# Eleven zero matmuls instead of 27 in the first gaps of TensorE

## The chip, the cores and the metric

The kernel runs on one core of one Trainium2 chip. The metric is the device time of one execution in microseconds. The core has five instruction streams: TensorE (PE; its weight loads are shown as PEld), VectorE (DVE), ScalarE (ACT), GpSimd (POOL) and SyncE (SP), which issues nearly all transfers here.

## What is computed

```
scores  = scale * x @ state^T          a  = softmax(scores)      xread = a @ state
scores2 = scale * state @ x^T          a2 = softmax(scores2)     sread = a2 @ x
y   = concat([xread, sread]) along the sequence, heads side by side   # 8 x (512 + 32) rows, 512 wide
out = maximum(y @ w1, y @ w2) @ w_out
```

There are 8 batches, 8 heads, 512 rows of x and 32 of state for each, 64 numbers a head; w1 and w2 are 512 x 1024, w_out is 1024 x 512. Inputs and output are f32, the products run in bf16.

## The kernel before, in words

maximum(h1, h2) is written as h2 + relu(h1 - h2). So the kernel forms w1 - w2 (the tile wd) and w2 @ w_out (the tile wwo) once, and multiplies both with the state of each batch (sw), so that the attention's probabilities (at) meet products of state and weights rather than the weights. For each batch of x there follow the first layer (l1, line 375), relu, and the second layer in quarters by a scheme of sums and differences (lines 426 and 432).

Weights, x and state come in pieces that SP issues in a fixed order: `ldx.b.g` is half of a batch of x, `ldw1.k`, `ldw2.k` and `ldwo.k` are quarters of the weights, each 256 x 512 numbers. The quarters that matter here come in the order ldw2.2, ldw2.3, ldwo.2, ldw1.3, ldwo.3, ldw1.2, ldw2.1, ldw2.0, ldwo.0, ldwo.1, ldw1.0, ldw1.1.

The first part of the program is an order written out by hand: the string ORDER, a list of tokens. Each token is one step on one engine, `name.args@banks` for TensorE with the PSUM banks that it writes, `name.args>engine` for the others. The loop that reads it issues one step after the other, so the order of the tokens on an engine is the order of its instructions. The steps that the text speaks of:

- `fill.k@bank`: one matmul of a tile of zeros (wz) into a bank. Nothing reads its result. With k of 100 and more it is 512 columns wide, else 256.
- `xt`, `S`, `at`: transposes of x (line 249), of the state (line 208) and of the probabilities a (line 291); `sc` are the scores (line 264), `srw` the state's read (line 321).
- `cwo`, `cw2`: casts of loaded weights to bf16; `w2` transposes a piece of w2 (line 548); `ww` is a part of w2 @ w_out (line 606).
- `sub.k.h`: half a piece of w1 - w2 (line 560); `sw.b.z` multiplies a part of wd or wwo with the state of batch b (line 352), and `swe` takes the result from its bank (line 102 on ACT, line 104 on DVE).

```
fill=lambda k, r: idle(1, r, 512 if k >= 100 else 256, k >= 200)

def idle(n, ring, w=512, f32=False):
    p = bank(ring)
    z = wz.bitcast(F32)[:, 0:256] if f32 else wz[:, 0:w]
    for j in range(n):
        nc.tensor.matmul(p[:, 0:z.shape[1]], z[:, 0:128], z, start=True, stop=True)
```

A matmul is two instructions in TensorE's stream, LDWEIGHTS and MATMUL. After the listed part, loops over the batches follow, which the change leaves as they are.

Of the kernel before, what the change touches and what calls it, by code (L numbers as in the profile page):

```python
# [20 lines left out]
CHUNKS = [[(0, 512), (512, 1024)], [(0, 512), (512, 1024)]]  # L21

ORDER = """
ldx.0.0 ldS.0.2 fill.10@0 ldx.0.1 fill.109@1 ldx.1.1 fill.114@0 fill.11@1 ldx.1.0 fill.110@0 ldw2.2 fill.100@1
fill.9@0 ldw2.3 fill.111@1 ldwo.2 fill.0@0 fill.5@1 fill.101@0 ldw1.3 ce.0.1>A ce.0.0>V ldwo.3 xt.0.0@0 cS.0.2>V
ldw1.2 fill.106@1 xte.0.0>V fill.105@2 ce.0.3>P ce.0.2>A ldw2.1 S.0.2@1 xt.0.1@2 ldw2.0 Se.0.2.1>A Se.0.2.0>V sc.0.0@1
xte.0.1>V fill.13@0 ldwo.0 fill.6@3 ce.1.2>P exp.0.0>A fill.115@4 fill.108@3 sc.0.1@4 ce.1.3>V ldwo.1 red.0.0>V
exp.0.1>A xt.1.1@3 ce.1.0>A ce.1.1>P srw.0@4,1 xte.1.1>V ldw1.0 mul.0.0>P swre.0.0>A red.0.1>V sc.1.1@3 xt.1.0@2
cw2.2>P exp.1.1>A ldw1.1 fill.15@4 fill.107@0 xte.1.0>V fill.1@4 swre.0.1>A fill.2@3 fill.14@0 fill.3@4 fill.112@3
cw2.3>A red.1.1>V mul.0.1>P fill.102@4 fill.7@3 ldx.2.0 fill.4@2 mul.1.1>V w2.3@2 cwo.2>A w2.2@3 w2e.3>V sc.1.0@4  # L30
at.0.0@0 at.0.1@1 exp.1.0>A w2e.2>V ww.3.2@2 ldx.2.1 ww.2.2@4 red.1.0>V sub.3.1>P ate.0.0>A srw.1@3,5 ate.0.1>A
mul.1.0>V cwo.3>A ww.0.2@1 sub.3.0>V at.1.0@0 at.1.1@6 swre.1.0>A ww.1.2@7 sub.2.0>V ate.1.1>A ldS.2.8 ww.3.3@2
ww.1.3@7 sub.2.1>V ate.1.0>A ww.0.3@1 swre.1.1>A sw.1.1@0,6 sw.0.1@5,3 swe.1.1.0>A swe.1.1.1>V ww.2.3@4 swe.0.1.0>A
swe.0.1.1>V l1.1.5@6 cw2.1>P srp.0>P srp.1>P l1.1.7@0 cw2.0>A re.1.5>V l1.0.7@3 w2.1@5 re.1.7>V re.0.7>A w2.0@6 w2e.1>V cwo.0>A
l1.0.5@3 l1.1.6@0 w2e.0>V l1.1.4@5 cwo.1>A ww.2.0@4 re.0.5>V ww.1.0@7 re.1.4>A ww.2.1@4 sub.0.0>V ww.1.1@7 re.1.6>A
sub.0.1>V ww.3.0@2 wwe.2>A ww.0.1@1 sub.1.1>V ww.3.1@2 wwe.1>A ww.0.0@1 sub.1.0>V wwe.3>A l1.0.4@7 wwe.0>A cb.2.0>P
sw.0.0@2,4 re.0.4>V wt.0>P sw.1.0@0,5 swe.0.0.0>A swe.0.0.1>V sw.0.w@1,3 sw.1.w@7,6 cb.2.1>P swe.1.0.0>A swe.1.0.1>V xtd.2 wt.1>P
p2.1@2 l1.0.6@4 swe.0.w.0>A re.0.6>V l1.0.3@0 l1.0.2@5 swe.0.w.1>A re.0.3>V swe.1.w.0>V mS.1>A
l1.0.1@4 l1.0.0@1 p2.0@3 swe.1.w.1>V mS.0>A Sd dif.0>P re.0.2>V re.0.1>A re.0.0>A p2o.0
l1.1.0@7 l1.1.1@6 l1.1.2@0 l1.1.3@5 re.1.0>V re.1.1>A re.1.2>A rs.0.0>V rs.0.1>V re.1.3>A  # L40
p2o.1 ldx.4.1 ldx.3.0 ldx.4.0 ldx.3.1
p1.0@1 k0.0>A p1.1@4 rs.0.2>V wt.2>V v00.0 p6.0 rs.0.3>V k0.1>A k1.0>A p5.0@7 wt.3>V v00.1 rs.1.0>V k2.0>A
sc.2.0@6 exp.2.0>A sc.2.1@0 exp.2.1>A sw.2.0@5,3 red.2.0>V mul.2.0>P red.2.1>V swe.2.0.0>A swe.2.0.1>A ce.2.0>A ce.2.1>A ce.2.2>A ce.2.3>A
p7.0 o7.0 v11.0 rs.1.1>V mul.2.1>P p3.0 o3.0 rs.1.2>V atd.2 sw.2.w@6,2 swe.2.w.0>A v01.0 swe.2.w.1>A
p4.0 o4.0 rs.1.3>V ce.3.0>P ce.3.1>P cb.3.0>P ce.3.2>P ce.3.3>P cb.3.1>P v10.0>A store.0 xtd.3 dif.1>P
sr.2@0 p6.1 k1.1>A sw.2.1@5,3 sre.2>V swe.2.1.0>A swe.2.1.1>V p5.1@7 k2.1>A
p7.1 o7.1 v11.1 p3.1 o3.1 v01.1 srt.2@0 srte.2>A p4.1 o4.1 v10.1>A ldx.5.0 ldx.5.1
"""

LATE = 2  # L50
# [851 lines left out]
```

## Time and profile before

| | |
|---|---|
| median of 3 runs | 145.04 us (145.03 to 145.11) |
| profiled execution | 144.88 us, of which 143.1 us from the first to the last instruction |
| mean granted clock of TensorE | 0.996 |
| PE busy | 134.7 us, 94% of the span |
| transfers | 29.50 MB, mean 206 GB/s |

The profile's times count from the first instruction. A row of the timeline reads: start, busy time, engine, line, operation, out<-in, shapes, count, and in brackets the idle time of the engine before it with what ended it. The chain of waits is followed back from the last instruction, and lists start, duration and work. In the rows of windows, an engine has its busy time and in brackets its count of instructions.

### The profile page before, as it was taken

The page shows a single profiled execution, that of the slowest core. Times are in us where ns is not written, and L with a number is a line of the kernel's source. Part 1 is how long each engine was busy: PE and PEld are TensorE (multiplying, and loading weights), DVE is VectorE, ACT ScalarE, POOL GpSimd, SP SyncE. Part 2 cuts the span into 40 slices and gives each one's busy share as a digit, 9 for nine tenths or more (in the row PEclk, how much of TensorE's full clock was granted, in tenths as well). Part 3 has the DMA queues.
Part 4 walks back from the last instruction along what each step waited for, and adds up shares of the span by engine and source line. Part 5 has one row for each costly group of instructions (what it writes and reads, how often), then busy time and mean ns, then how long its engine had stood idle before and what let it go on. Part 6 is the DMA issues. An engine that isn't in the chain of part 4 may idle for free.

```text
span 143.1 us, 3680 instructions
## 1 busy us (share of the span) xinstructions
PE 134.7 (94%) x1448; PEld 95.4 (67%) x1458; DVE 108.3 (76%) x197; ACT 86.9 (61%) x168; POOL 72.1 (50%) x99
## 2 busy tenths in 40 slices
PE   6889989999999999999999999999999999999980
PEld 2467725456787776786778477747876786788860
DVE  3488959868999938997899799669948997847420
ACT  4367589895689535855682769086726855753220
POOL 4147326099009993399269908971990464200000
PEclk9999999999999999999999999999999999999998
DMA  3999999945997979949995999759137042502073
GB/s 112 342 366 392 384 386 386 343 83 93 196 343 230 286 180 249 236 42 293 242 386 109 212 355 195 160 213 211 35 65 293 2 58 82 234 5 73 9 248 119
DMA packets 36452, 29.50 MB, mean 206 GB/s; under 512 B 22608, under 2 KB 32336, under 8 KB 35536
## 3 DMA queue, kind: packets, MB, share of 16 engines
q1 hardware_dynamic: 36160, 29.10, 70.8%
q8 instruction: 12, 0.20, 0.6%
q10 hardware_dynamic: 272, 0.13, 0.3%
q14 instruction: 8, 0.07, 0.1%
HBM read 15.20 MB, written 8.91 MB: 169 GB/s over the span
## 4 chain that ended last, share of the span: by engine, by line
PE 83%; DMA 11%; ACT 1%; issue 1%; DVE 0%; SPq 0%; DVEq 0%
PE bank L426 36%; PE bank L375 19%; PE bank L432 10%; DMA big<-in_moe_w_out_dram 8%; PE bank L352 5%; DMA big<-in_x_dram 4%; PE bank L606 3%; PE bank L473 2%; PE bank L515 2%; PE bank L264 2%; PE bank L304 2%; PE bank L513 1%; ACT wo L102 1%; PE bank L548 1%; PE bank L336 0%
## 5 line engine op out<-in xcount | busy, mean ns | idle before, releaser
L102 ACT COPY big<-bank 128x512 f32<-128x512 f32 (+2 forms) x40 | 21.9, 551 | 16.6 <-PE bank L426 8.4
L280 POOL TENSOR_TENSOR a<-e,er 128x512 bf16<-128x512 bf16 x14 | 16.7, 1209 | 29.5 <-ACT e L272 18.0
L370 DVE TENSOR_SCALAR r<-bank 128x512 bf16<-128x512 f32 x32 | 21.9, 690 | 11.7 <-PE bank L375 10.6
L375 PE MATMUL bank<-at,sw 128*128 128x512 bf16 x120 | 29.1, 379 | 0.6 <-DVE sw L104 0.2
L426 PEld LDWEIGHTS <-big 128*128 128x128 bf16 x256 | 23.9, 98 | 6.3 <-DVE er L277 2.1
L426 PE MATMUL bank<-big,big 128*128 128x256 bf16 x192 | 23.1, 273 | 0.1
L102 ACT CAST sw<-bank 128x512 bf16<-128x512 f32 x36 | 20.1, 608 | 3.2 <-PE bank L352 3.2
L375 PEld LDWEIGHTS <-sw 128*128 128x128 bf16 x128 | 12.2, 98 | 13.5 <-ACT sw L102 0.5
L368 ACT ACTIVATE r<-bank 128x512 bf16<-128x512 f32 x32 | 18.3, 597 | 4.9 <-PE bank L375 4.7
L426 PEld LDWEIGHTS <-r 128*128 128x128 bf16 x192 | 18.2, 98 | 3.8 <-issue 0.5
L402 DVE TENSOR_TENSOR big<-bank,big 128x512 f32<-128x512 f32 (+1 forms) x25 | 16.4, 660 | 5.4 <-PE bank L432 5.4
L106 POOL CAST xe<-big 128x512 bf16<-128x512 f32 x23 | 16.5, 749 | 6.1 <-DMA big<-in_x_dram 6.1
L426 PE MATMUL bank<-wo,r 128*128 128x256 bf16 x128 | 16.3, 273 | 0.0
L102 ACT COPY sread_t<-bank 128x128 bf16<-128x128 bf16 x8 | 3.2, 472 | 18.7 <-PE bank L336 15.5
L106 POOL CAST xb<-big 128x1024 bf16<-128x1024 f32 x12 | 12.2, 1035 | 4.7 <-DMA big<-in_x_dram 4.7
L432 PE MATMUL bank<-sw,at 128*128 128x256 bf16 x96 | 14.4, 273 | 0.0
L432 PEld LDWEIGHTS <-at 128*128 128x128 bf16 x128 | 12.5, 98 | 1.7
L402 DVE TENSOR_TENSOR big<-r 128x1024 bf16<-128x1024 bf16 x16 | 12.6, 788 | 0.6
L276 DVE TENSOR_REDUCE sums<-e 128x16 f32<-128x512 bf16 x16 | 10.6, 660 | 0.3 <-ACT e L272 0.2
L272 ACT ACTIVATE e<-bank 128x512 bf16<-128x512 f32 x16 | 8.9, 601 | 1.3 <-PE bank L264 1.3
L402 POOL TENSOR_TENSOR big<-sw 128x512 bf16<-128x512 bf16 x8 | 9.2, 1151 | 0.9 <-POOL a L280 0.9
L104 DVE CAST sw<-bank 128x512 bf16<-128x512 f32 x12 | 7.9, 679 | 0.6 <-PE bank L352 0.6
(100 smaller groups left out, 188.7 us busy)
## 6 DMA issues: line engine op xcount, KB each, us to landing
big<-in_x_dram SPq DMA_DIRECT2D x14, 512.0 KB, 6.2
out_dram<-big SPq DMA_DIRECT2D x7, 1024.0 KB, 5.3
big<-in_moe_w_dram SPq DMA_DIRECT2D x8, 512.0 KB, 12.0
big<-in_moe_w_out_dram SPq DMA_DIRECT2D x4, 512.0 KB, 11.6
big<-in_x_dram SPq DMA_DIRECT2D x1, 1024.0 KB, 6.9
out_dram<-big SPq DMA_DIRECT2D x4, 256.0 KB, 2.6
sf<-in_state_dram SPq DMA_DIRECT2D x1, 384.0 KB, 10.4
out_dram<-w2m SPq DMA_DIRECT2D x2, 128.0 KB, 2.5
```

What stands on the lines that cost most here:

```text
L102: nc.scalar.copy(o, i)
L104: nc.vector.tensor_copy(o, i)
L106: nc.gpsimd.tensor_copy(o, i)
L272: nc.scalar.activation(out=e_view(e_s[b % 2], hh).rearrange("p (g c) i n -> p g c (i n)", g=2), in_=p.rearrange("p (c g m) -> p g c m", c= ...
L276: nc.vector.tensor_reduce(es_all[:, b, hh], e_view(e_s[b % 2], hh), axis=AXX, op=ALU.add)
L280: (nc.gpsimd if eng == "P" else nc.vector).tensor_mul(e_view(a_s[b % 2], hh), e_view(e_s[b % 2], hh), er_s[b % 2][:, hh].unsqueeze(3).to_b ...
L368: nc.scalar.activation(out=o, in_=p, func=ACTF.Relu)
L370: nc.vector.tensor_scalar(o, p, scalar1=0.0, scalar2=None, op0=ALU.max)
L375: nc.tensor.matmul(p, sw_s[b % 3][:, g, f * 128:(f + 1) * 128], at_s[b % 3][:, g].rearrange("p c t -> p (c t)"), start=(g == 0), stop=(g = ...
L402: (nc.gpsimd if eng == "P" else nc.vector).tensor_tensor(o, i0, i1, op=op)
L426: nc.tensor.matmul(pv[c], lhs[:, f, 128 * c:128 * c + 128], rhs[:, f, :], start=first and f == 0 and (c == 0 or pv.split), stop=False, ski ...
L432: nc.tensor.matmul(pv[c], at_s[b % 3][:, g, 2 * i + c, :], rhs[:, g, :], start=False, stop=False, skip_group_check=True)
```

## The change

The order has eleven fills instead of 27, all of 512 columns: eight ahead of the first transposes of x (before: eleven, of both widths), none between these and the state's (before: two), one between the scores (before: four), and two instead of ten ahead of the transposes of the first pieces of w2. All other tokens stand in the same order, and the streams of the other engines are unchanged. The first lines of the table:

```
-ldx.0.0 ldS.0.2 fill.10@0 ldx.0.1 fill.109@1 ldx.1.1 fill.114@0 fill.11@1 ldx.1.0 fill.110@0 ldw2.2 fill.100@1
+ldx.0.0 ldS.0.2 fill.100@0 ldx.0.1 fill.101@1 ldx.1.1 fill.102@0 fill.103@1 ldx.1.0 fill.104@0 ldw2.2 fill.105@1
...
```

In TensorE's stream, the last gap: between the transposes of x (xe1) and those of w2 (wb1 is the cast piece) stood, before, ten fills; the first ones and the last one are shown.

```order
L249 MATMUL bank2_65<-ident0_71,xe1_85 128x128
L575 LDWEIGHTS wz0_73
L575 MATMUL bank4_67<-wz0_73 128x256
L575 LDWEIGHTS wz0_73
L575 MATMUL bank0_63<-wz0_73 128x512
...
L575 MATMUL bank2_65<-wz0_73 128x256
L548 LDWEIGHTS wb1_108
```

Now there are two there (the numbers of the lines are three lower, since the table is three lines shorter):

```order
L246 MATMUL bank2_65<-ident0_71,xe1_85 128x128
L572 LDWEIGHTS wz0_73
L572 MATMUL bank3_66<-wz0_73 128x512
L572 LDWEIGHTS wz0_73
L572 MATMUL bank4_67<-wz0_73 128x512
L545 LDWEIGHTS wb1_108
```

Eight matmuls, 16 instructions, are gone from between the two; another eight are gone from the gaps ahead.

The 256th instruction: before, it was the first weight load of the product w2 @ w_out (w2m0 is the transposed w2), just behind the transposes of the probabilities of batch 0 (a0).

```order
L291 LDWEIGHTS a0_93
L291 MATMUL bank1_64<-ident0_71,a0_93 128x128
L606 LDWEIGHTS w2m0_80
L606 MATMUL bank2_65<-wo0_77,w2m0_80 128x512
L606 LDWEIGHTS w2m0_80
```

Now it is among the transposes of batch 1's probabilities (a1), behind the third group of the weight product:

```order
L603 LDWEIGHTS w2m0_80
L603 MATMUL bank1_64<-wo0_77,w2m0_80 128x512
L288 LDWEIGHTS a1_94
L288 MATMUL bank0_63<-ident0_71,a1_94 128x128
L288 LDWEIGHTS a1_94
```

The boundary of 256 has moved by 32 instructions of the work, over four matmuls of the weight product, the state's read of batch 1, two more of the weight product and two transposes.

More of the change, by code (lines that the diff above doesn't have):

```diff
@@ L23 @@
 ORDER = """
-ldx.0.0 ldS.0.2 fill.10@0 ldx.0.1 fill.109@1 ldx.1.1 fill.114@0 fill.11@1 ldx.1.0 fill.110@0 ldw2.2 fill.100@1
[L25 to L44, printed above, removed]
@@ L45 @@
-p4.0 o4.0 rs.1.3>V ce.3.0>P ce.3.1>P cb.3.0>P ce.3.2>P ce.3.3>P cb.3.1>P v10.0>A store.0 xtd.3 dif.1>P
-sr.2@0 p6.1 k1.1>A sw.2.1@5,3 sre.2>V swe.2.1.0>A swe.2.1.1>V p5.1@7 k2.1>A
-p7.1 o7.1 v11.1 p3.1 o3.1 v01.1 srt.2@0 srte.2>A p4.1 o4.1 v10.1>A ldx.5.0 ldx.5.1
+ldx.0.0 ldS.0.2 fill.100@0 ldx.0.1 fill.101@1 ldx.1.1 fill.102@0 fill.103@1 ldx.1.0 fill.104@0 ldw2.2 fill.105@1
+fill.106@0 ldw2.3 fill.107@1 ldwo.2 ldw1.3 ce.0.1>A ce.0.0>V ldwo.3 xt.0.0@0 cS.0.2>V ldw1.2 xte.0.0>V ce.0.3>P
+ce.0.2>A ldw2.1 S.0.2@1 xt.0.1@2 ldw2.0 Se.0.2.1>A Se.0.2.0>V sc.0.0@1 xte.0.1>V ldwo.0 ce.1.2>P exp.0.0>A fill.108@4
@@ new lines @@
+sc.0.1@4 ce.1.3>V ldwo.1 red.0.0>V exp.0.1>A xt.1.1@3 ce.1.0>A ce.1.1>P srw.0@4,1 xte.1.1>V ldw1.0 mul.0.0>P
+swre.0.0>A red.0.1>V sc.1.1@3 xt.1.0@2 cw2.2>P exp.1.1>A ldw1.1 xte.1.0>V swre.0.1>A fill.109@3 fill.110@4 cw2.3>A
+red.1.1>V mul.0.1>P ldx.2.0 mul.1.1>V w2.3@2 cwo.2>A w2.2@3 w2e.3>V sc.1.0@4 at.0.0@0 at.0.1@1 exp.1.0>A w2e.2>V
+ww.3.2@2 ldx.2.1 ww.2.2@4 red.1.0>V sub.3.1>P ate.0.0>A srw.1@3,5 ate.0.1>A mul.1.0>V cwo.3>A ww.0.2@1 sub.3.0>V
+at.1.0@0 at.1.1@6 swre.1.0>A ww.1.2@7 sub.2.0>V ate.1.1>A ldS.2.8 ww.3.3@2 ww.1.3@7 sub.2.1>V ate.1.0>A ww.0.3@1
@@ new lines @@
+swre.1.1>A sw.1.1@0,6 sw.0.1@5,3 swe.1.1.0>A swe.1.1.1>V ww.2.3@4 swe.0.1.0>A swe.0.1.1>V l1.1.5@6 cw2.1>P srp.0>P
+srp.1>P l1.1.7@0 cw2.0>A re.1.5>V l1.0.7@3 w2.1@5 re.1.7>V re.0.7>A w2.0@6 w2e.1>V cwo.0>A l1.0.5@3 l1.1.6@0 w2e.0>V
+l1.1.4@5 cwo.1>A ww.2.0@4 re.0.5>V ww.1.0@7 re.1.4>A ww.2.1@4 sub.0.0>V ww.1.1@7 re.1.6>A sub.0.1>V ww.3.0@2 wwe.2>A
+ww.0.1@1 sub.1.1>V ww.3.1@2 wwe.1>A ww.0.0@1 sub.1.0>V wwe.3>A l1.0.4@7 wwe.0>A cb.2.0>P sw.0.0@2,4 re.0.4>V wt.0>P
+sw.1.0@0,5 swe.0.0.0>A swe.0.0.1>V sw.0.w@1,3 sw.1.w@7,6 cb.2.1>P swe.1.0.0>A swe.1.0.1>V xtd.2 wt.1>P p2.1@2 l1.0.6@4
@@ new lines @@
+swe.0.w.0>A re.0.6>V l1.0.3@0 l1.0.2@5 swe.0.w.1>A re.0.3>V swe.1.w.0>V mS.1>A l1.0.1@4 l1.0.0@1 p2.0@3 swe.1.w.1>V
+mS.0>A Sd dif.0>P re.0.2>V re.0.1>A re.0.0>A p2o.0 l1.1.0@7 l1.1.1@6 l1.1.2@0 l1.1.3@5 re.1.0>V re.1.1>A re.1.2>A
+rs.0.0>V rs.0.1>V re.1.3>A p2o.1 ldx.4.1 ldx.3.0 ldx.4.0 ldx.3.1 p1.0@1 k0.0>A p1.1@4 rs.0.2>V wt.2>V v00.0 p6.0
+rs.0.3>V k0.1>A k1.0>A p5.0@7 wt.3>V v00.1 rs.1.0>V k2.0>A sc.2.0@6 exp.2.0>A sc.2.1@0 exp.2.1>A sw.2.0@5,3 red.2.0>V
+mul.2.0>P red.2.1>V swe.2.0.0>A swe.2.0.1>A ce.2.0>A ce.2.1>A ce.2.2>A ce.2.3>A p7.0 o7.0 v11.0 rs.1.1>V mul.2.1>P
@@ L48 @@
+p3.0 o3.0 rs.1.2>V atd.2 sw.2.w@6,2 swe.2.w.0>A v01.0 swe.2.w.1>A p4.0 o4.0 rs.1.3>V ce.3.0>P ce.3.1>P cb.3.0>P
+ce.3.2>P ce.3.3>P cb.3.1>P v10.0>A store.0 xtd.3 dif.1>P sr.2@0 p6.1 k1.1>A sw.2.1@5,3 sre.2>V swe.2.1.0>A swe.2.1.1>V
+p5.1@7 k2.1>A p7.1 o7.1 v11.1 p3.1 o3.1 v01.1 srt.2@0 srte.2>A p4.1 o4.1 v10.1>A ldx.5.0 ldx.5.1
 """
```

## The prediction

> **What bounds the kernel now.** I read the page's busy shares and slices first, to see whether there is one limit or several stages.
>
> ```profile
> span 143.1 us, 3680 instructions
> PE 134.7 (94%) x1448; PEld 95.4 (67%) x1458; DVE 108.3 (76%) x197; ACT 86.9 (61%) x168; POOL 72.1 (50%) x99
> PE   6889989999999999999999999999999999999980
> DMA  3999999945997979949995999759137042502073
> ```
>
> PE (TensorE's matmuls) is busy 94% of the span, and from the seventh slice on (a slice is 3.58 us, so from about 21 us) it is full to the end. The only thin slices are the first six, and there the DMA row stands at 9. So two stages: about 21 us in which the loads set the pace, and 120 us in which TensorE does. A change in the first gaps is worth what it does to the moment at which the full stretch begins. For that I read the chain of waits in order of time, at that border.
>
> ```profile
> 6.55 11.23 DMA big<-in_moe_w_out_dram
> ...
> 17.81 1.05 ACT wo L102
> ...
> 18.91 1.46 PE bank L606 x6
> 20.36 0.47 PE bank L352 x8
> ...
> 21.66 1.46 PE bank L375 x6
> ```
>
> The chain runs from a load of moe_w_out (the token ldwo.3, landed at 6.55 + 11.23 = 17.78) through its cast on ACT to six matmuls of the weight product, to the products with the state (sw.1.1), and, by their eviction, to the first matmuls of the first layer (l1.1.5) at 21.66. After that the chain is TensorE's own. I then read the timeline of the same stretch for what else ends there.
>
> ```profile
> 13.75 1.04 ACT L102 CAST wo<-big 128x1024 bf16<-128x1024 f32 x1 [0.30 <-DMA big<-in_moe_w_out_dram]
> 15.16 1.27 POOL L560 TENSOR_TENSOR wd<-big,big 128x512 bf16<-128x512 f32 x1 [1.73 <-DMA big<-in_moe_w_dram]
> 17.09 0.69 DVE L560 TENSOR_TENSOR wd<-big,big 128x512 bf16<-128x512 f32 x1
> 17.81 1.04 ACT L102 CAST wo<-big 128x1024 bf16<-128x1024 f32 x1 [1.41 <-DMA big<-in_moe_w_out_dram]
> 18.99 1.29 DVE L560 TENSOR_TENSOR wd<-big,big 128x512 bf16<-128x512 f32 x2 [1.22 <-DMA big<-in_moe_w_dram]
> 20.29 0.26 PEld L352 LDWEIGHTS <-sbd 64*32 64x32 bf16 x16 [0.42 <-DVE wd L560]
> ```
>
> The last row matters most: sw.1.1 starts at 20.29 because DVE's difference of the weights (sub.2.0 and sub.2.1, 18.99 + 1.29 = 20.28) is then ready, and that waited for another load, ldw1.2. So two loads end at the same place. TensorE's path (18.91 plus six matmuls) reaches it at about 20.2 and DVE's at 20.28; the second is the one that lets sw.1.1 go.
>
> **What the instruction fetch does now.** The loads come in the order wo.2, w1.3, wo.3, w1.2, and their users were waiting, so the rows above give their landings: 13.75, 15.16, 17.81, 18.99. The pieces are of one size (256 x 512 numbers of f32); the steps are 1.41, 2.65 and 1.18 us. Between the second and the third about 1.3 us went missing. The DMA rows show what else was on the engines: a queue, its packets, their MB and their share of sixteen engines. The four rows are of four stretches: the whole run, 15.5 to 15.6 us, 15.6 to 29.6 (whose answer names no instruction queue), and 0 to 62.5.
>
> ```profile
> q8 instruction: 12, 0.20, 0.6%
> q8 instruction: 1, 0.02, 65.4%
> q1 hardware_dynamic: 4314, 5.08, 107.6%
> q8 instruction: 5, 0.08, 0.6%
> ```
>
> One instruction packet of some 16 KB starts between 15.5 and 15.6 us and holds one of the sixteen DMA engines for 0.654 x 16 x 0.1 = 1.05 us; from 15.6 to 29.6 there is no other. I read it so: a load is spread over all engines and has landed when the last share of it has, so one engine that is a microsecond late makes every later load late, and it doesn't catch up while its queue is full. That fits the 1.3 us, and that the step after it is no shorter than 1.18. TensorE itself does not stop there:
>
> ```profile
> 15.09 1.03 PE L606 MATMUL bank<-wo,w2m 128*128 128x512 bf16 x4
> 15.95 1.07 PE L321 MATMUL bank<-xe,e 128*128 128x260 bf16 x8
> ```
>
> No idle time stands ahead of either row. So the price of this fetch is paid by wo.3 and w1.2 and what comes behind.
>
> How far ahead of TensorE is a fetch sent? The counts of weight loads (PEld, each with one matmul) in three stretches tell where TensorE stood.
>
> ```profile
> 0.00:15.53 15.53, 12.68 (x129) 8.41 (x131) 10.01 (x22) 8.79 (x16) 6.78 (x27) 1.00 0.91 310
> 0.00:62.40 62.40, 58.52 (x585) 38.77 (x591) 49.03 (x85) 43.62 (x79) 33.18 (x57) 1.00 0.88 264
> ```
>
> At the first fetch TensorE was at 2 x 131 = 262, just over 256. At the fifth (five packets by 62.5) it was at 2 x 591 = 1182, where five times 256 is 1280: the packet ran almost 100 instructions ahead of TensorE. So I take it that a fetch is asked for when the sequencer, well ahead of the array, comes to the boundary, and that the packet then queues in its DMA engine. Among the loads (share 107.6%) it queues longer, which is why the first one came only with the 262nd.
>
> **The change part by part.** Sixteen fewer zero matmuls, and the eleven that stay are all 512 wide.
>
> ```profile
> 1.29 3.81 PE L575 MATMUL bank<-wz 128*128 128x256 bf16 x11 [1.29 <-DVE ones L578]
> 5.03 0.78 PE L249 MATMUL bank<-ident,xe 128*128 128x128 bf16 x8
> 5.64 0.59 PE L575 MATMUL bank<-wz 128*128 128x512 bf16 x2
> 6.08 0.39 PE L208 MATMUL bank<-ident,sb 128*128 128x128 bf16 x4
> 7.23 0.62 PE L249 MATMUL bank<-ident,xe 128*128 128x128 bf16 x8 [0.77 <-ACT xe L102]
> 8.44 0.81 PE L575 MATMUL bank<-wz 128*128 128x256 bf16 x4
> 11.77 1.57 PE L575 MATMUL bank<-wz 128*128 128x256 bf16 x9
> 13.50 1.07 PE L548 MATMUL bank<-ident,wb 128*128 128x128 bf16 x16 [0.16 <-ACT wb L102]
> 17.22 0.50 PEld L291 LDWEIGHTS <-a 128*128 128x128 bf16 x8 [0.27 <-DVE a L280]
> 17.29 0.61 PE L291 MATMUL bank<-ident,a 128*128 128x128 bf16 x8
> 17.73 0.59 PE L606 MATMUL bank<-wo,w2m 128*128 128x512 bf16 x2
> 18.91 1.46 PE L606 MATMUL bank<-wo,w2m 128*128 128x512 bf16 x6 [0.58 <-ACT wo L102]
> ```
>
> First gap: 11 matmuls with 4352 columns become 8 with 4096. They end some 0.2 us sooner and the transposes of x still wait for DVE's cast at 5.03: nothing. Second gap: the two zeros at 5.64 go (0.43 us up to 6.08); the state's transposes behind them can start 0.4 us sooner, but the next ones wait for ACT until 7.23, so nothing. Third gap, four become one (1536 columns become 512), so the second scores come up to 0.4 us sooner. Fourth gap, ten become two: the time to 13.50 is idle instead. At 13.50 TensorE waits for ACT's cast of a loaded weight in both kernels, which swallows the 0.4 us. So as work the sixteen cost nothing and bring nothing; the cover is the loads.
>
> What remains is the fetch, which comes later by what 32 instructions take there. Low end: if it is asked for 100 to 128 instructions ahead, only 16 of the 32 have been taken out before that place and TensorE passes it 0.1 to 0.7 us later than before. If it is asked for about 96 ahead, the place falls on the wait at 13.50 (before, just ahead of the zeros at 11.77): about 2 us later. High end: if it follows the 256th instruction itself, that moves from 15.09 to the transposes of a at 17.29: 2.2 us later. The packet's start goes from 15.5 to between 15.6 and 17.7. I take the middle, 16 to 17, by the row of the fifth fetch, which shows a lead near 100.
>
> What that gives: wo.3 has its other shares in by about 17.81 - 1.3 = 16.5. A packet after that leaves wo.3 alone and its cast runs at 16.5 instead of 17.81. But w1.2 would be through only at 18.99 - 1.3 = 17.7, and a packet anywhere before that still makes it land at about 18.97. DVE then still starts at 18.99, sw.1.1 at 20.29, l1.1.5 at 21.66. The six matmuls of wo.3 are done earlier and TensorE idles in front of sw.1.1 instead. Sum: 0 to -0.1 us for the path, 0 for the work. The profiled execution took 144.88 us around a span of 143.1; the median of the runs is 145.04, and the forecast is **145.0 us**, on the scale of the median.
>
> One rule of the Trainium skill speaks against any effect: "Runtime: NRT & Kernel Launch", section Instruction fetch mechanics, says that the sequencer streams blocks of 16 KiB, 256 instructions, and that crossing a boundary costs one tail bump, mostly hidden. The trace agrees for TensorE and shows a cost of 1.3 us for the loads beside it, which that section does not count; by the rule the time stays at 145.04, by the loads' cost it comes to the sum above.
>
> **The rivals.** *Faster: the fetch clears w1.2 too.* If the packet starts after 17.7, both loads land 1.3 us sooner. DVE is free at 17.09 + 0.69 = 17.78 and has the difference by 17.78 + 1.29 = 19.07. ACT's cast runs 16.5 to 17.55. TensorE has its transposes at 17.29, two matmuls at 17.73, and six more from 18.17 on, as 0.43 us for each two from 5.64 to 6.08 (the tail left out), to 19.46. So sw.1.1 goes at 19.46 instead of 20.29, 0.83 us sooner. Not all is kept, because later loads are late all the same:
>
> ```profile
> 25.84 2.61 DVE L560 TENSOR_TENSOR wd<-big,big 128x512 bf16<-128x512 f32 x4 [0.28 <-DMA big<-in_moe_w_dram]
> 29.12 0.54 PEld L352 LDWEIGHTS <-sbd 64*32 64x32 bf16 x25 [0.42 <-issue]
> ```
>
> The last pieces of w1 give their differences by 25.84 + 2.61 = 28.45, and sw.0.0 needs them; it now starts at 29.12. So 0.6 us at most survives: 145.04 - 0.6 = 144.4. For it: the bare count puts the 256th at 17.29, and the first packet came 0.5 us after that place before. Against it: the fifth packet ran ahead.
>
> *Slower: TensorE's clock falls in the wider gaps.* The zeros keep TensorE busy; the opening eleven cost 3.81 us for 4352 columns, or 0.43 us for 512, where six matmuls at 18.91 take 0.24 us each with the tail of the last in it: half speed at first, full by 5.64 (two in 0.59). The rise takes up to 4.35 us. If the clock fell before 13.50, up to 4.35 us of work would run at half speed, a loss of 2.2 us, less the 0.85 us of idle time between 13.50 and 20.29 (0.58 at 18.91, 0.27 at 17.22): about 1.3 us, 146.3. It decides when an idle gap is long enough. Idle grows from 0.77 us at most to 1.2 (5.64 + 0.39 = 6.03 to 7.23) and at most 1.3 (11.77 + 0.43 to 13.50); 0.77 us did not do it, and nothing in this trace tests 1.2. The Trainium skill ("TensorE: Matmul & The Clock Gate", Part 1) puts the fall after an idle window of about 3.4 us; by that neither gap reaches it. The run before shows no fall.
>
> *The fetch does not move at all* (the low end, 0.1 us): the time is that of the forecast, and it counts there.
>
> **How the numbers follow.** Forecast with the unmoved fetch 0.72, its own range 144.8 to 145.2; faster by the cleared load 0.18; slower by the clock 0.10. The range leaves out the slower case and the far end of the others: 144.35 to 145.3. A measurement of this kernel tells about 0.2%, 0.29 us; the faster case is 0.6 us and the slower one 1.3, so the three chances are 0.18, 0.72 and 0.10.
>
> **What would show it.** In the changed kernel: one instruction packet in 15.6 to 17.7; the cast of wo.3 at 16.5 to 17.8; DVE's difference still at about 18.99 and sw.1.1 still at 20.29, with TensorE idle in front of it; the chain now through moe_w1 instead of moe_w_out. The prediction is wrong if DVE's row starts near 17.8 (the fetch cleared w1.2), if matmuls of zeros or transposes after 5.64 show the long durations of the opening, or if sw.0.0 at 29.12 moves by more than 0.2 us.

## The result, and the profile after

The changed kernel takes 146.45 us (median; 146.34 to 146.74), the kernel before 145.07 us (144.86 to 145.5). The ratio is 1.0093, 95% interval 1.0075 to 1.011: slower by 1.35 us. The profiled execution took 146.34 us around a span of 144.6, at a granted clock of 0.998. Its page, from the span, the busy shares and the groups:

```profile
span 144.6 us, 3648 instructions
PE 132.7 (92%) x1432; PEld 93.6 (65%) x1442; DVE 108.8 (75%) x197; ACT 87.5 (61%) x168; POOL 72.0 (50%) x99
L372 PE MATMUL bank<-at,sw 128*128 128x512 bf16 x120 | 29.1, 379 | 2.3 <-DMA at<-a 1.7
```

PE is busy 2.0 us less (132.7 against 134.7), which is the zeros that are gone, and the span is 1.5 us longer. The group that reads the probabilities (L372, before L375) costs the same 29.1 us of work, 379 ns a matmul, but the idle time ahead of it has grown from 0.6 to 2.3 us, and the releaser of 1.7 of it was not in that row before: a DMA that writes at.

**The first stretch went better than forecast.** The instruction packet now starts in 17.4 to 17.5 us (the row of that stretch, read as in the prediction: 0.655 x 16 x 0.1 = 1.05 us on one engine):

```profile
q8 instruction: 1, 0.02, 65.5%
```

The timeline after, in the order of time, where before the cast of wo.3 stood at 17.81, DVE's difference at 18.99, sw.1.1 at 20.29 and l1.1.5 at 21.66:

```profile
16.55 1.04 ACT L99 CAST wo<-big 128x1024 bf16<-128x1024 f32 x1
17.20 2.00 DVE L557 TENSOR_TENSOR wd<-big,big 128x512 bf16<-128x512 f32 x3
19.66 0.14 PEld L349 LDWEIGHTS <-sbd 64*32 64x32 bf16 x16 [0.42 <-DVE wd L557]
21.01 1.24 PE L372 MATMUL bank<-at,sw 128*128 128x512 bf16 x5 [0.18 <-DVE sw L101]
28.58 0.62 PE L349 MATMUL bank<-wd,sbd 64*32 64x512 bf16 x16
```

Both loads are early: the cast of wo.3 runs 1.26 us sooner, and DVE makes all three differences in one piece from 17.20 to 19.20, so that sw.1.1 goes 0.63 us sooner, l1.1.5 0.65 us and sw.0.0 (the last row) 0.54 us. The packet's cost has not gone, it has moved: by the landing records the loads come 1.2 to 1.4 us apart but for one step, which was the one up to wo.3 (15.09 to 17.79 us) and is now the one behind w1.2, up to w2.1 (17.88 to 20.27). The lead of TensorE is still there when the loops over the batches run. The same matmuls of the second layer, after and then before:

```profile
38.34 1.91 PE L423 MATMUL bank<-big,big 128*128 128x256 bf16 x16
```

```profile
38.88 1.91 PE L426 MATMUL bank<-big,big 128*128 128x256 bf16 x16
```

**Then two microseconds are lost at two places.** The chain of waits after holds two long pieces that the chain of before does not have:

```profile
61.45 4.92 DMA at<-a
66.41 0.38 PE bank L372
...
115.99 4.76 DMA at<-a
120.79 0.38 PE bank L372
```

In the loops the probabilities of a batch are no longer turned by TensorE but by DMA: SP issues one transposing transfer from a to at (line 282, before 285). In two batches TensorE now waits for it. PE's rows of the timeline, after:

```profile
66.41 0.81 PE L372 MATMUL bank<-at,sw 128*128 128x512 bf16 x2 [0.79 <-DMA at<-a]
...
120.79 0.81 PE L372 MATMUL bank<-at,sw 128*128 128x512 bf16 x2 [0.89 <-DMA at<-a]
```

And the same matmuls before, with no wait ahead of either:

```profile
66.00 1.24 PE L375 MATMUL bank<-at,sw 128*128 128x512 bf16 x4
...
119.33 1.46 PE L375 MATMUL bank<-at,sw 128*128 128x512 bf16 x5
```

The lead of 0.54 us has become a lag of 66.41 - 66.00 = 0.41 us at the first place, a loss of 0.95, and a lag of 120.79 - 119.33 = 1.46 us at the second, a further loss of 1.05. Sum: -0.54 + 0.95 + 1.05 = +1.46 us, the difference of the spans (144.6 - 143.1). Nothing else is needed.

Why were these two transfers late? The DMA rows give each issue with its time to landing. Before, in the stretches 61.4 to 62.1 and 115.5 to 116.1 us (the instruction packet is in the second):

```profile
at<-a SPq DMA_TRANSPOSE x1, 3.6
...
q8 instruction: 1, 0.02, 11.7%
at<-a SPq DMA_TRANSPOSE x1, 3.5
```

After, in the same two stretches, and then in 64.3 to 64.4 and 118.6 to 118.7:

```profile
at<-a SPq DMA_TRANSPOSE x1, 4.9
...
at<-a SPq DMA_TRANSPOSE x1, 4.8
...
q8 instruction: 1, 0.02, 57.8%
...
q8 instruction: 1, 0.02, 55.4%
```

An instruction packet of TensorE starts in both transfers in both kernels: the fifth and the tenth packet of the twelve. Before, they start at 62.41 and 115.81 us, 0.42 and 0.25 us after the issue of the transposes. After, they start at 64.34 and 118.69, 2.89 and 2.70 us after it, and the transposes land 1.2 to 1.3 us later. The profile has sixteen landing records for each transfer, which I take for the shares of the sixteen engines: after, fifteen of them come 3.0 to 3.3 us after the issue and the last one at 4.8 to 4.9.

### The profile page after: what moved, and what is told of

It is laid out like the page before. It is cut to its first block, busy times and chain, and to the rows that moved or that the text cites. A ratio compares the mean times of both kernels' runs of the same rounds, so it can differ in the third digit from the quotient of the medians.

```text
span 144.6 us, 3648 instructions
## 1 busy us (share of the span) xinstructions
PE 132.7 (92%) x1432; PEld 93.6 (65%) x1442; DVE 108.8 (75%) x197; ACT 87.5 (61%) x168; POOL 72.0 (50%) x99
## 4 chain that ended last, share of the span: by engine, by line
PE 76%; DMA 13%; ACT 4%; SPq 2%; issue 2%; DVE 0%; POOL 0%; DVEq 0%
PE bank L423 29%; PE bank L372 19%; PE bank L429 8%; DMA at<-a 7%; DMA big<-in_moe_w_dram 6%; PE bank L603 4%; PE bank L349 4%; PE bank L470 2%; PE bank L512 2%; PE bank L261 2%; ACT sw L99 2%; PE bank L545 1%; ACT big L99 1%; SPq L164 1%; PE bank L510 1%
## 5 line engine op out<-in xcount | busy, mean ns | idle before, releaser
L372 PE MATMUL bank<-at,sw 128*128 128x512 bf16 x120 | 29.1, 379 | 2.3 <-DMA at<-a 1.7
L372 PEld LDWEIGHTS <-sw 128*128 128x128 bf16 x128 | 12.3, 98 | 15.4 <-issue 2.1
```

The costliest lines, as they stand in the source:

```text
L372: nc.tensor.matmul(p, sw_s[b % 3][:, g, f * 128:(f + 1) * 128], at_s[b % 3][:, g].rearrange("p c t -> p (c t)"), start=(g == 0), stop=(g = ...
```

## The experiments

The theory to be tested, "position": the time is set by where each 256th instruction of TensorE falls, early (among the loads) and late (in the transposes of a), and what is done in the first gaps is of no weight. Its rivals: the zeros matter as work (a clock that falls, gaps that are no longer filled), or the loop suffers because it begins half a microsecond sooner ("early start"), or the late transfers differ from execution to execution and have nothing to do with the count. For them the kernels have a new token, `pad.n@bank`: n matmuls of zeros of 64 columns, two instructions each. Unless another base is named, the edits are made to the changed kernel. Each ratio is to the kernel before, with its 95% interval.

**1. The count as before, the zeros narrow.** Sixteen narrow matmuls stand where the sixteen were removed:

```
-ldwo.2 ldw1.3
+ldwo.2 pad.1@0 pad.1@1 pad.1@0 ldw1.3
... (two in the second gap, three in the third, eight in the fourth)
```

> The eleven wide zeros stay, and sixteen zeros of 64 columns stand where the sixteen were taken out. The count of instructions is that of the kernel before, the array's work that of the changed kernel plus 16 x 64 columns. Theory (position): what costs is where the later instruction fetches fall; with the old count the first packet starts at 15 to 16 us, the fifth and tenth miss the transposes of a, and the time is 145.05 within 0.3. Rival 1 (activity): the idle gaps or the missing zeros themselves cost, through the clock or otherwise: 146.4. Rival 2 (early start): the loop suffers because it begins 0.55 us sooner; here it does not: 145.05.

145.22 us, ratio 1.0007 (0.9996 to 1.0019). The first packet is back at 15.07 us, TensorE never waits for a transpose, and the timeline shows the loads late again:

```profile
18.03 1.04 ACT L99 CAST wo<-big 128x1024 bf16<-128x1024 f32 x1 [1.47 <-DMA big<-in_moe_w_out_dram]
19.38 1.29 DVE L557 TENSOR_TENSOR wd<-big,big 128x512 bf16<-128x512 f32 x2 [1.46 <-DMA big<-in_moe_w_dram]
20.51 0.36 PEld L349 LDWEIGHTS <-sbd 64*32 64x32 bf16 x16 [0.42 <-DVE wd L557]
```

The sixteen pads have 1024 columns where 4608 were taken out. So the zeros' width, their work, is worth nothing that shows; their number is worth both the gain and the loss.

**2. The number given back after the early gain.** Sixteen pads behind the first packet, so that it stays late while all the later ones come at their old counts:

```
-swe.0.1.1>V l1.1.5@6
+swe.0.1.1>V pad.16@0 l1.1.5@6
```

> The changed kernel with sixteen zeros of 64 columns put in just ahead of l1.1.5, so behind the first fetch. The first fetch stays at 17.4, the later ones go back to the instructions at which they stood before. The sixteen take about 0.45 us, of which TensorE has 0.3 to 0.4 idle there. Theory (position): no wait on the transposes of a, 144.5 to 145.0. Rival 1 (activity): 146.4. Rival 2 (early start): the loop still begins up to 0.55 us sooner, 146.3 to 146.9.

144.77 us, ratio 0.9987 (0.9966 to 1.0007); the profiled execution 144.35 around 142.6. No wait for a transpose is left, and the early gain stays, as two rows of its timeline show:

```profile
17.07 2.04 DVE L557 TENSOR_TENSOR wd<-big,big 128x512 bf16<-128x512 f32 x3
19.53 0.14 PEld L349 LDWEIGHTS <-sbd 64*32 64x32 bf16 x16 [0.42 <-DVE wd L557]
```

Adding 16 matmuls that do nothing takes 1.7 us off the changed kernel. Against the kernel before no gain shows in the time (the interval holds 1): the pads take back most of the early lead. The rows separate the two effects of the change: the early one is a gain, the late ones are the loss.

**3. No zeros at all.**

```
-fill.100@0 ... fill.110@4   (all eleven)
```

> No zeros at all, 22 instructions fewer than in the changed kernel. Theory (position): the later fetches fall another 1.2 us or so behind the point at which they hurt, the transposes of a have then landed, so no wait on them: 144.5, plus what a slow clock in the opening costs where the loads do not hide it (0 to 1 us). Rival 1 (activity): slower still than the changed kernel, 146.5 to 148. Rival 2 (early start): 146.4.

146.92 us, ratio 1.0129 (1.0112 to 1.0146). Here the theory's forecast of the late packets missed: the tenth still starts 2.70 us after the issue and its transfer takes 4.77. By its time alone the run sides with the rival of the zeros' work (146.5 to 148). The waits and the timeline show what cost it:

```profile
PE bank L372 <- DMA at<-a: 1.5, 2, 0.9
PE bank L246 <- DVE xe L101: 5.0, 1, 5.0
...
11.99 0.61 PE L246 MATMUL bank<-ident,xe 128*128 128x128 bf16 x8
```

TensorE starts 5 us late and slow: the eight transposes that take 0.61 us at 11.99 take 1.04 in the first row of PE's timeline, at 4.98. At the loop's start it is only about 0.2 us ahead of the kernel before, where the changed kernel was 0.54. And there is a second wait for transposes, 0.65 us at 93.38: all sixteen shares of that transfer land late, at 4.08 to 4.28 us, with the seventh packet starting 0.20 us ahead of the issue. The run does not tell the theories apart, since a slow opening and a moved count come together. It does show that a packet does not move smoothly with the count: with 22 instructions fewer than in the changed kernel, the tenth stands where it stood.

**4. Half of the pads.** `pad.8@0` at the place of experiment 2.

> As the run with sixteen, but eight zeros of 64 columns ahead of l1.1.5. The fifth and tenth fetch move back by 16 instructions, about 1 us, to some 2 us after the issue of the transposes instead of 2.8. Theory (position): between 144.5 (if only the last microsecond of a transpose can be hurt) and 146.4 (if all of it can). Rivals 1 and 2: 146.4.

145.08 us, ratio 1.0016 (0.9996 to 1.0036): within the theory's range and against both rivals, with one wait of 0.5 us for a transpose in the profile. Its fifth packet starts 1.32 us after the issue, and all of that transfer's shares are late (4.66 us). The profiled execution (145.86, clock 0.982) also shows what the prediction's slower rival named. Rows of two stretches; behind the busy times stands the granted clock:

```profile
5.00:9.00 4.00, 2.81 (x37) 2.07 (x37) 2.40 (x6) 1.68 (x5) 1.20 (x2) 1.00 1.04 343
9.00:12.60 3.60, 3.23 (x27) 2.69 (x28) 2.47 (x5) 1.60 (x4) 2.84 (x4) 0.54 1.01 374
```

The clock falls to 0.54 in the second, after a stretch in which PE was busy for 2.81 of 4.00 us. In the profile of the changed kernel, which has the same tokens up to there, PE was busy for 2.41 of the same 4.00 us and the clock stayed at 1.00.

**5 and 6. More pads.** `pad.24@0` and `pad.20@0` at the same place.

> As the run with sixteen narrow zeros ahead of l1.1.5, with twenty-four. The fifth and tenth fetch come some 0.4 to 0.9 us sooner still, at or just ahead of the issue of the transposes of a. Theory (position): no wait on these transposes, and fewer executions in which one is hit by chance; the eight more cost 0.22 us: 144.8 to 145.0. Rival 2 (early start): 146.4 or more. Against both: if a fetch just ahead of the issue hurts as well, 145.5 to 146.

> As the run with sixteen, with twenty narrow zeros ahead of l1.1.5. Theory (position): no wait on the transposes, 144.7 to 144.9, between the runs with sixteen and twenty-four. Rival 2 (early start): 146.4 or more.

146.81 us (145.76 to 149.94; the ratio, 1.0123 with 1.0079 to 1.0167, leaves out the execution at 149.94) and 146.1 us (1.0093, 1.0062 to 1.0123): a miss. The fifth and the tenth packet are harmless as forecast, but now the ninth is not: it starts 2.71 and 2.74 us after the issue of its batch's transposes, these take 4.95 and 4.96 us, and each profile has this row of waits:

```profile
PE bank L372 <- DMA at<-a: 1.0, 1, 1.0
```

I had looked at two packets where all have to be placed. The row explains 1.0 us; the pads' own work (24 of them 0.7 us, from 21.45 to 22.14) and loads that land 0.8 and 0.4 us later in these profiles than in that of experiment 2 are the rest. Those loads are late from the first piece of the weights on (ldw2.2 lands at 11.78 and 11.38 us, in experiment 2 at 11.02), ahead of anything that the edit touches; so this is a difference between executions, and its cause is open. The time with 24 pads lies in the range of the early start, but the loop starts at 39.37 us here, 0.49 us later than in the kernel before (38.88), so it is not that.

**7. Pads late, ahead of the tenth packet alone.** Sixteen matmuls of 64 columns in the loop, in the batch with index 4:

```
+if b == 4:
+    for _ in range(16):
+        nc.tensor.matmul(banks[BZ][:, 0:64], ident, ident[:, 0:64], start=True, stop=True)
```

> The changed kernel with sixteen matmuls of the identity, 64 columns each, put into the loop over batches at batch 4, after its second scores: between the fifth and the tenth fetch. They cost at most 0.45 us. Theory (position): the fifth fetch still hits the transposes (0.97 us lost, as in the changed kernel), the tenth comes 2.5 us sooner and misses them: 146.45 - 1.04 + 0.45 = 145.9. Rival 2 (early start) and any theory in which the count ahead of the tenth does not matter: 146.45 + 0.45 = 146.9.

146.23 us, ratio 1.0077 (1.0054 to 1.0101). Inconclusive: in the profile (146.19, clock 0.982) the tenth packet is at +0.42 us and harmless, as meant, but so is the fifth, at +2.68 with a landing of 3.19, which the theory took for a hit. The time went elsewhere: the loop starts 0.5 us behind the kernel before, where the changed kernel was 0.54 us ahead (the clock fell to 0.56 in 9.0 to 12.6 us of this profile), about 0.6 us go in two pieces at 52 to 58 us, and the pads take 0.5. That the tenth packet moved and its wait went is as forecast; that the same start of the fifth does no harm here is not.

**8. The decisive one: four pads in the kernel before.** The base is the kernel before, with its 27 zeros. By experiments 5 and 6 eight more instructions bring its ninth packet into a bad place. The edit adds `pad.4@0` ahead of l1.1.5, about 0.1 us of work.

> The kernel before with all its 27 zeros, and four zeros of 64 columns put in ahead of l1.1.5: eight instructions more, some 0.1 us of work. The first fetch stays where it was. Theory (position): as in the runs with twenty and twenty-four narrow zeros, the ninth fetch comes to start some 0.2 us later behind the issue of its transposes of a (2.7 instead of 2.5 us), hits their last packets and costs about 1.2 us: 146.1 to 146.4. Rivals in which zeros, gaps or the early start matter and the count does not: 145.05 to 145.2.

146.14 us, ratio 1.0076 (1.0054 to 1.0098): slower by 1.2 us, as the position theory says and against the rivals. Chance from execution to execution is out too: the six lie at 145.87 to 146.39, seventeen of the kernel before, taken with them, at 144.59 to 145.52. Before, the transposes of that batch (the stretch 102.2 to 102.3) and the packet (104.8 to 104.9):

```profile
at<-a SPq DMA_TRANSPOSE x1, 3.4
...
q8 instruction: 1, 0.02, 70.0%
```

With the four pads, the stretches 102.4 to 102.7 and 105.1 to 105.2, and the row of waits:

```profile
at<-a SPq DMA_TRANSPOSE x1, 5.0
...
q8 instruction: 1, 0.02, 71.8%
...
PE bank L372 <- DMA at<-a: 1.0, 1, 1.0
```

Both packets take the same time on their engine (0.700 and 0.718 x 1.6 = 1.12 and 1.15 us), but one starts 2.54 us after the issue and the other 2.74, and the transfer behind the second lands 1.6 us later. The section Instruction fetch mechanics of the Trainium skill's "Runtime: NRT & Kernel Launch" calls the crossing of a block mostly hidden. In this run it is not: four matmuls with 0.1 us of work cost 1.2 us through it.

**9. Two pads fewer than in experiment 2.** `pad.14@0`.

> The changed kernel with fourteen narrow zeros ahead of l1.1.5, 25 in all. Theory (position): fifth and tenth fetch still ahead of the transposes' packets, ninth as before, 144.6 to 144.9. Rival 2 (early start): 146.4.

144.68 us (144.38 to 146.15), ratio 0.9993 (0.9969 to 1.0017). No gain over experiment 2 that the intervals show. Of the executions above 145.0, three of four had a granted clock of 0.981 to 0.984.

**10 and 11. The early gap filled again.** Two wide zeros ahead of the state's transposes, with `pad.14@0` (27 in all); then a third one ahead of the second scores, with `pad.13@0`:

```
-S.0.2@1
+fill.111@1 fill.112@2 S.0.2@1
...
-swe.0.1.1>V l1.1.5@6
+swe.0.1.1>V pad.14@0 l1.1.5@6
```

> The changed kernel with two wide zeros put back ahead of the state's transposes, where two stood before, and fourteen narrow ones ahead of l1.1.5: 27 in all. Theory (position): the first fetch comes four instructions sooner than in the changed kernel, 17.0 to 17.4, still behind wo.3 and w1.2; the later ones as before; 144.5 to 144.8. If the slow executions of the runs with fourteen and sixteen narrow zeros (0.981 to 0.984 of the clock in most) come from a clock that falls in the wider gap at 5.6 to 7.2 us, the highest time comes down from 146.1 to 145.3 or less; if not, it stays near 146.

> As the run before it, with one more wide zero between the first scores and thirteen narrow ones, 27 in all. The first fetch another two instructions sooner. Theory (position): 144.5 to 144.8 if it still clears w1.2; 145.0 if it does not. The same on the spread.

144.55 us (144.31 to 145.01), ratio 0.9974 (0.9963 to 0.9985), and 144.51 us (144.23 to 145.03), ratio 0.9976 (0.9966 to 0.9987). Both beat the kernel before by 0.4 us and the changed kernel by 1.9. The first packet starts at 17.17 and 17.20 us and w1.2 lands at 17.71 and 17.78, not delayed, and the highest times come down as expected. The mean granted clock was under 0.99 in none of these 24 executions and in none of 83 of the kernel before; in the seven kernels whose opening is that of the changed kernel it was so in 21 of 62 (3 of 12 in experiment 9, 7 of 11 in experiment 4). The first of the two, by its page, with the start of the loop:

```profile
span 142.5 us, 3691 instructions
PE 135.0 (95%) x1458; PEld 94.7 (66%) x1458; DVE 108.6 (76%) x197; ACT 87.1 (61%) x168; POOL 72.0 (51%) x99
...
38.33 0.81 PE L423 MATMUL bank<-big,big 128*128 128x256 bf16 x6
```

The span is 0.6 us shorter than before with the same number of matmuls (PE's busy times can't be compared to 0.3 us: the profile before lacks the records of ten matmuls). The loop starts as early as in the changed kernel (38.33 and 38.34 us) and the time is 1.9 us lower, which rules out the early start. The kernel that wins has as many zeros as the one it beats: 13 of them wide and in the first gaps, 14 narrow and behind the first packet.

**The positions side by side.** All packets that start 2.4 to 3.0 us after the issue of a transfer at<-a, and three that start earlier, from the DMA records of the profiled executions: start and end of the packet and the landing, in us after the issue of the transposes.

| kernel, packet | packet | landing | wait of TensorE |
|---|---|---|---|
| before, 5th | from 0.42 | 3.60 | none |
| before, 10th | from 0.25 | 3.52 | none |
| experiment 4, 5th | 1.32 to 2.85 | 4.66 | 0.5 |
| before, 9th | 2.54 to 3.66 | 3.40 | none |
| experiments 1, 2, 7, 9 and 10, 9th | from 2.50 to 2.54 | 3.38 to 3.45 | none |
| experiment 11, 9th | 2.66 to 3.83 | 3.44 | none |
| experiment 3, 5th | 2.67 to 3.98 | 3.13 | none |
| experiment 7, 5th | 2.68 to 3.79 | 3.19 | none |
| after, 9th | 2.70 to 3.86 | 3.43 | none |
| experiment 4, 9th | 2.84 to 3.93 | 3.42 | none |
| after, 10th | 2.70 to 3.58 | 4.76 | 0.9 |
| experiment 3, 10th | 2.70 to 3.59 | 4.77 | 0.9 |
| experiments 5, 6 and 8, 9th | 2.71 to 3.86, 2.74 to 3.89 (twice) | 4.95, 4.96, 4.96 | 1.0 each |
| after, 5th | 2.89 to 3.81 | 4.92 | 0.8 |

Of the packets that start at 2.4 us or later there are two groups and nothing between. In the hits (the six transfers with a wait of 0.8 to 1.0 us) the last share lands 1.07 to 1.18 us after the packet's end and 1.5 to 1.6 us behind the fifteen others; in the spared ones the last share is in before the packet ends. That looks like a queue in which the packet has come ahead of a last part of the transposes, or behind it. The start alone does not decide it: no packet before 2.70 us was a hit of this kind, but two at 2.70 and 2.84 were spared. Transfers of which all the shares land late together are another matter: experiment 4's fifth, experiment 3's seventh (4.28), and experiment 7's third (packet from 0.08, landing 4.89, no wait). What delays those isn't shown. What decides between harm and none stays open, since the records don't name the engine that a packet uses. That the packet causes the late landing, rather than coming along with it, rests on the 1.1 us behind its end in every hit, on experiment 8, where four pads were all that changed, and on the waits that go and return with the count in 2, 5 and 6.

## Why the prediction was wrong

*The zeros as work: nothing.* Right. Experiment 1 has nearly the width of the changed kernel, the old number, and the old time. The opening zeros ended 0.6 us sooner (1.29 + 3.23 = 4.52 for 5.10) instead of the 0.2 of the working, and the transposes behind them still began at 5.00.

*The packet's start: between 15.6 and 17.7, "I take the middle, 16 to 17, by the row of the fifth fetch, which shows a lead near 100".* This choice failed first. The packet started at 17.43, near the high end, 1.9 us later than before. The first packet follows the bare count: before, it came 0.4 us behind the product at 15.09 in which the 256th instruction stood, and now it comes with the transposes of a in which that instruction stands, by PE's timeline after:

```profile
17.40 0.61 PE L288 MATMUL bank<-ident,a 128*128 128x128 bf16 x8
```

One row was taken for a rule: by the same count the packets two to eleven of the kernel before start between 10 instructions behind TensorE (the third) and 98 ahead of it (the fifth, the one that was read). The one row that bore on the place itself, the first packet of the kernel before, had no lead.

*What that gives: w1.2 still late, DVE at 18.99, sw.1.1 at 20.29.* Wrong with it. DVE's row starts at 17.20 with the piece that was ready before, its second piece at 17.90 (the refutation said "near 17.8"), and sw.0.0 moved by 0.54 us: two of the three signs that were named as refutations. The mechanism that came true is that of the rival called faster, and its sizes were close: sw.1.1 at 19.66, where the rival had 19.46, and 0.54 us kept, where it had at most 0.6. It said that w1.2 is cleared by a packet after 17.7; 17.43 was enough: the load landed at 17.88, while the packet held its engine to 18.48, so a share of it on that engine must have been through when the packet began.

*The later fetches: not in the sum.* This is the step that set the sign. The prediction quotes "12" packets and places the fifth, and prices the move of the first alone; yet 32 instructions fewer move all twelve. The late ones had been costed at nothing without a word, and two of them are worth +0.95 and +1.05 us. With this term the sum would have been 145.04 - 0.54 + 2.00 = 146.5; measured 146.45. The rows that could have warned were there: before, TensorE reads the two transfers 4.01 and 3.77 us after their issue, and they land at 3.60 and 3.52, so 0.41 and 0.25 us of delay are all that is free; and a packet lies in each. What they could not give is which place does harm, so the term would have had to stand as a bound, with the first packet's 1.3 us as its nearest row: nothing to about 1 us for each packet that comes to lie in a transfer.

*The slower rival: the clock falls, 146.3.* Right time, wrong mechanism. The profiled execution after had a clock of 0.998 and 146.34 us, and two executions at 0.987 took 146.37 and 146.6, about the median. In other kernels with the same gaps the clock does fall in some executions (0.54 and 0.56 in the profiles of experiments 4 and 7), so the rival's condition was a real one; it isn't what this change costs. "TensorE: Matmul & The Clock Gate" of the Trainium skill, Part 1, puts the fall after an idle window of about 3.4 us. The rows of experiment 4 differ: 0.54 in 9.0 to 12.6 us, after PE had been idle for 1.19 us in all of the 4.00 us ahead, 0.82 us at most in one piece.

*"The fetch does not move at all".* Refuted by the packet at 17.43.

## What to carry to other kernels

Adding or removing instructions on an engine moves every later block of its instruction stream, not only the next one: list all the packets, and for each the transfers that are in flight where it lands now and where it will land. Where an edit moves a packet to a better place, give the count back right behind it (14 to 16 narrow matmuls here), so that the rest of the program keeps its positions; and when a kernel with fewer instructions and less work becomes slower, look at the landing times of its transfers before looking at its engines. Conversely, a change of a few matmuls that seems to gain or lose 1% may be this effect and nothing in its own idea.

## What the runs showed of the hardware

- One instruction packet of some 16 KB holds a DMA engine for 0.9 to 1.5 us, and what waits for all sixteen engines can pay for it in full: the cast of wo.3 ran 1.26 us sooner without it, and a transposing transfer landed 1.2 to 1.6 us later with it.
- For a packet that starts 2.5 to 2.9 us after the issue, the cost to such a transfer was all or nothing in seventeen cases: landing at 3.1 to 3.5 us or at 4.8 to 5.0, with packets of the changed kernel that start 0.01 us apart on either side.
- How far a packet runs ahead of TensorE is no constant. Counted as in the prediction (twice the weight loads begun, from k times 256), the fifth and tenth packet of the kernel before start 98 and 88 instructions ahead of it, the same two of the changed kernel, which hit, 30 and 20; the third of the kernel before starts 10 behind it. A request that waits until the transposes are through with the engine would look like that; this is an inference from the counts, and no run tested it.
- TensorE's clock fell to 0.54 behind idle gaps of at most 0.82 us, while the changed kernel's profile, with the same opening and a gap of 1.25 us, kept 1.00. With that opening the mean clock was under 0.99 in 21 of 62 executions, with two or three more wide matmuls in the first gaps in none of 24. That the fill is the cause is likely, not shown: the kernel without zeros had none either, in five executions. Nor is the clock all of the spread, since the highest time of experiment 2, 146.06, came at a clock of 1.0.
